# A layer norm's first root on ScalarE, a third gate tile in halves, and a moved y product, in a scan-plus-FFN kernel whose VectorE order comes from two virtual clocks

## The chip, the cores and the metric

The kernel runs on one core of a Trainium2 chip. The metric is the device time in microseconds (us) of the whole program; "span" is the time from the first to the last instruction in the hardware profile of one execution, some 2 us shorter than the device time. Engines are written as the profile has them: PE is TensorE, PEld its weight loads, DVE VectorE, ACT ScalarE, POOL GpSimd.

## The reference

```python
xn = layernorm(x)                                  # x: 1 x 2048 x 512, bf16
Bu = einsum("bld,pd->blp", xn, B_bar)              # complex
for t in range(2048):
    h = Lam_bar * h + Bu[:, t, :]                  # 512 complex states
y = 2 * real(einsum("blp,dp->bld", hs, C)) + xn * Dskip
f = (gelu(xn @ w_gate) * (xn @ w_up)) @ w_down     # 512 -> 1376 -> 512
return x + y * silu(f)
```

## The kernel before

The 2048 tokens are worked through in four slabs of 512. The complex scan is made real by rotating: VectorE multiplies the input `U` by cosine and sine tables (`pp`, `qq`, combined to `Wt`), scans in real arithmetic (`Ft`), and rotates back (`pp`, `qq`, combined to `hst`). TensorE then makes `y` of a 128-token block from `hst` and `C`, eight matmuls of 512 columns: the first four read the real half of `hst`, two per half of the states, so that the third matmul is the first to need states that were rotated last. TensorE executes in the order of the program; a slab is eleven "gate steps" (a gate tile and an up tile each), and the y of the slab before are put between certain gate steps.

The head of the kernel:

```python
dummies(9)                                    # TensorE warm-up matmuls, 512 columns each
pt_ps = psum.tile(...); nc.tensor.transpose(pt_ps, pv, ident)     # small parameters
dummies(5)                                    # five more
ACT(out=pf, in_=pt_ps, func=AF.Copy)
...
for m in range(2): bn(0, m)                   # VectorE: statistics of token blocks 0, 1
bn_end(0, 0); bn_end(0, 1)
rstd(0, 0, 2)                                 # VectorE: + eps; GpSimd: ** -0.5
bn(0, 2); bn(0, 3)
xs = [norm0(0), norm0(1)]
...
tps = [t_xn0(0, xs[0]), t_xn0(1, xs[1])]      # TensorE transposes of the normalised blocks
xnT_out(nc.vector, 0, tps[0])                 # copies out of PSUM
xnT_out(nc.scalar, 1, tps[1], 0, KT // 2)
xnT_out(nc.vector, 1, tps[1], KT // 2, KT)
SPLIT = 2                                     # gate/up tiles 0 and 1 are made in token halves
```

And the layer that decides VectorE's order. It keeps two virtual clocks while the program is written; an operation put into `later` is pulled out when the clock says that it fits before the next one:

```python
clk = {"pe": 0.0, "dve": 0.0}
waiting = []
def pe_takes(n, one=0.2157): clk["pe"] += n * one
def pop():
    r, c, f, _ = waiting.pop(0)
    clk["dve"] = max(clk["dve"], r) + c
    f()
def drain(t, late):
    while waiting and max(clk["dve"], waiting[0][0]) + waiting[0][1] <= t + late: pop()
def dve(ready, cost, f, late=0.8):
    drain(ready, late)                        # what fits goes ahead
    clk["dve"] = max(clk["dve"], ready) + cost
    f()
def later(ready, cost, f, key=None): waiting.append((ready, cost, f, key))
...
def ln_small(s):                              # four small statistics of slab 3
    def f(): ...
    dve(now() + 1.0, 0.3, f)
...
Y_AT = {1: (7, 8, 9, 10), 2: (2, 3, 4, 5), 3: (2, 4, 6, 8)}   # gate steps with a y
XN_AT = {1: 1, 2: 2}
clk["pe"] = 8.3                               # the two starting clocks
clk["dve"] = 10.6
```

## Time and profile before

| what | value |
|---|---|
| time, median of 6 runs | 184.6 us (184.21 to 184.93) |
| span of the profiled run | 182.5 us |
| TensorE busy | 175.9 us |
| VectorE busy | 168.0 us |
| TensorE's only wait for `hst` | 0.73 us, at the first y of slab 1 |

In a timeline a row is: start, length, engine, line, operation, output<-inputs, shapes and the number of instructions; brackets tell how long the engine was idle just before and what ended that. The prediction shows the main rows. One view that it doesn't show also belongs here, TensorE's timeline of the first 7 us of the kernel before:

```profile
1.18 3.99 PE L150 MATMUL w_ps<-warm 128*128 128x512 bf16 x9 [1.18 <-DVE halfpi L126]
...
5.21 1.25 PE L150 MATMUL w_ps<-warm 128*128 128x512 bf16 x5
6.39 0.72 PE L178 MATMUL tp<-ident,xn 128*128 128x128 bf16 x8
```

From 1.18 us to the first transposes at 6.39 this view shows no gap and names no wait, but it doesn't tell what the transposes stood behind, because ends of matmuls are modelled. Starts tell it. Five warm-ups of 0.216 from 5.21 on leave TensorE free at 6.29, and the transposes start 0.45 after the normalisation (5.94); in e8 below, where a wait for `xn` is named, the distance is 0.47. So the normalised block came last here, and the warm-ups were only 0.1 ahead of it: a block that is 0.42 earlier would have found TensorE still at its warm-ups.

### The profile page before, as it was taken

How to read it: one execution, taken by the hardware profiler on the slowest of the kernel's cores; microseconds unless marked ns; L12 is line 12 of the kernel's file. 1: busy time of each engine (PE TensorE's matmuls, PEld its weight loads, DVE VectorE, ACT ScalarE, POOL GpSimd, SP SyncE). 2: the span in 40 equal slices, each digit the busy share in tenths (PEclk: the TensorE clock that was granted, in tenths of full speed). 3: DMA queues.
4: the chain of work that ended last, by engine and by line, in shares of the span. 5: the costliest groups of instructions: out<-in, count | busy, mean ns of one | idle time of the engine just before them, and what ended most of it. 6: DMA issues, size and time to landing. Idle time of an engine off the chain costs nothing.

```text
span 182.5 us, 2411 instructions
## 1 busy us (share of the span) xinstructions
PE 175.9 (96%) x831; PEld 82.8 (45%) x847; DVE 168.0 (92%) x266; ACT 112.5 (62%) x196; POOL 18.5 (10%) x44
## 2 busy tenths in 40 slices
PE   7899999999999999999998999999999999999992
PEld 2564444544444444544443444444444444444451
DVE  4988899999998899999999999999999999999493
ACT  3199997778899943267889455767428444472200
POOL 3668300700000000000004000000000000000000
PEclk9999999999999999999999999999999999999999
DMA  5999595691001400023000032200000001000002
GB/s 146 323 356 157 93 239 105 184 252 31 0 0 29 81 5 32 29 64 108 0 0 4 29 83 63 57 2 4 0 0 0 0 29 34 29 29 0 0 29 86
DMA packets 25643, 12.37 MB, mean 68 GB/s; under 512 B 15808, under 2 KB 25632, under 8 KB 25632
## 3 DMA queue, kind: packets, MB, share of 16 engines
q1 hardware_dynamic: 25456, 12.16, 27.6%
q8 instruction: 6, 0.10, 0.2%
q10 hardware_dynamic: 176, 0.07, 0.1%
q14 instruction: 5, 0.04, 0.1%
HBM read 6.46 MB, written 2.10 MB: 47 GB/s over the span
## 4 chain that ended last, share of the span: by engine, by line
PE 60%; DVE 22%; ACT 8%; DMA 4%; SPq 3%; issue 1%
PE f_ps L478 16%; PE up_ps L231 12%; PE g_ps L231 12%; PE y_ps L493 10%; PE u_ps L377 9%; DVE Ft L423 5%; DMA x_tok<-in_A_x_dram 4%; DVE qq L393 3%; ACT xn L582 3%; DVE pp L393 3%; ACT ub L466 2%; ACT gt L465 2%; DVE hst L397 2%; DVE yg L515 2%; DVE Wt L397 1%; DVE st L158 1%
## 5 line engine op out<-in xcount | busy, mean ns | idle before, releaser
L231 PE MATMUL up_ps<-xnT,wu 128*128 128x512 bf16 (+2 forms) x184 | 45.5, 370 | 0.2
L231 PE MATMUL g_ps<-xnT,wg 128*128 128x512 bf16 (+2 forms) x178 | 44.8, 369 | 0.8 <-ACT xnT L199 0.5
L465 ACT ACTIVATE gt<-g_ps 128x512 bf16<-128x512 f32 (+1 forms) x44 | 27.1, 616 | 22.1 <-PE g_ps L231 18.1
L478 PE MATMUL f_ps<-wd,at 128*128 128x512 bf16 (+1 forms) x172 | 38.5, 379 | 0.2
L466 ACT ACTIVATE ub<-up_ps 128x512 bf16<-128x512 f32 (+1 forms) x44 | 27.2, 618 | 7.3 <-PE up_ps L231 7.3
L423 DVE TENSOR_TENSOR_SCAN Ft<-rho,it,Wt 128x512 bf16<-128x512 f32 x24 | 29.5, 1269 | 0.0
L493 PE MATMUL y_ps<-C,hst 128*128 128x512 bf16 x117 | 27.9, 379 | 0.7 <-DVE hst L397 0.6
L377 PE MATMUL u_ps<-xnT,BT 128*128 128x512 bf16 x125 | 28.3, 379 | 0.2
L231 PEld LDWEIGHTS <-wg 128*128 128x128 bf16 (+1 forms) x184 | 18.3, 100 | 20.4 <-issue 0.5
L231 PEld LDWEIGHTS <-wu 128*128 128x128 bf16 (+1 forms) x184 | 18.4, 100 | 19.6
L478 PEld LDWEIGHTS <-at 128*128 128x128 bf16 (+1 forms) x176 | 17.2, 98 | 20.8
L382 ACT ACTIVATE U<-u_ps 128x512 bf16<-128x512 f32 x32 | 19.0, 615 | 8.3 <-PE u_ps L377 8.3
L377 PEld LDWEIGHTS <-BT 128*128 128x128 bf16 x128 | 12.5, 98 | 15.0
L483 ACT ACTIVATE g<-f_ps 128x512 f32<-128x512 f32 x16 | 9.6, 598 | 14.6 <-PE f_ps L478 14.6
L493 PEld LDWEIGHTS <-hst 128*128 128x128 bf16 x120 | 11.7, 98 | 15.0 <-DVE hst L397 1.3
L471 DVE TENSOR_TENSOR at<-gt,ub 128x1024 bf16<-128x1024 bf16 x20 | 13.5, 679 | 0.6 <-ACT ub L466 0.6
L397 DVE TENSOR_TENSOR hst<-pp,qq 128x1024 bf16<-128x1024 bf16 x16 | 10.5, 689 | 0.2
L397 DVE TENSOR_TENSOR Wt<-pp,qq 128x1024 bf16<-128x1024 bf16 x16 | 10.5, 688 | 0.2
L158 DVE BATCH_NORM_STATS2 st<-x_tok 128x6 f32<-128x512 bf16 x12 | 7.5, 682 | 3.4 <-DMA x_tok<-in_A_x_dram 3.3
L582 ACT ACTIVATE xn<-x_tok,nb,rs 128x512 bf16<-128x512 bf16 x12 | 10.3, 859 | 0.0
L515 DVE TENSOR_TENSOR yg<-yt,g 128x512 bf16<-128x512 f32 x14 | 9.7, 692 | 0.6
L393 DVE TENSOR_TENSOR pp<-U,cos_b 128x2048 bf16<-128x2048 bf16 x8 | 9.8, 1223 | 0.2
(111 smaller groups left out, 152.7 us busy)
## 6 DMA issues: line engine op xcount, KB each, us to landing
out_dram<-ot SPq DMA_DIRECT2D x15, 128.0 KB, 1.7
x_tok<-in_A_x_dram SPq DMA_DIRECT2D x3, 512.0 KB, 5.4
wd<-in_B_w_down_dram SPq DMA_DIRECT2D x1, 1280.0 KB
wg<-in_B_w_gate_dram SPq DMA_DIRECT2D x2, 384.0 KB
wu<-in_B_w_up_dram SPq DMA_DIRECT2D x2, 384.0 KB, 6.7
wg<-in_B_w_gate_dram SPq DMA_DIRECT2D x1, 352.0 KB
wu<-in_B_w_up_dram SPq DMA_DIRECT2D x1, 352.0 KB, 4.0
x_tok<-in_A_x_dram SPq DMA_DIRECT2D x2, 128.0 KB, 2.2
```

What stands on the lines that cost most here:

```text
L231: nc.tensor.matmul(ps[:fs, a:b], lhsT=w[:, kt, fsl], rhs=xnT[:, kt, s * TS + a : s * TS + b], start=(kt == 0), stop=(kt == KT - 1),)
L377: nc.tensor.matmul(u_ps[:, :], lhsT=BT[:, ri, kt, pt * P : (pt + 1) * P], rhs=xnT[:, kt, cols], start=(kt == 0), stop=(kt == KT - 1),)
L382: ACT(out=U[:, ri, q, :], in_=u_ps[:, :], func=AF.Copy)
L393: TT(out=box[key][:], in0=src()[:], in1=tab[:, hs, :].unsqueeze(1).to_broadcast(W), op=ALU.mult)
L397: return lambda: TT(out=dst()[i], in0=box["pp"][:, i, :, :], in1=box["qq"][:, 1 - i, :, :], op=op)
L423: nc.vector.tensor_tensor_scan(out=box["F"][:, ri, q, :], data0=rho[:, pt : pt + 1].to_broadcast([P, TS]), data1=box["W"][:, ri, q, :], in ...
L465: ACT(out=gt[:fs, i, :], in_=g_ps[:fs, :], func=AF.Gelu_apprx_tanh)
L466: ACT(out=ub[:fs, i, :], in_=u_ps[:fs, :], func=AF.Copy)
L471: dve(now() + lag, 0.63, lambda: TT(out=at[:, j - 1 : j + 1, :], in0=gt[:], in1=ub[:], op=ALU.mult))
L478: nc.tensor.matmul(f_ps[:, :], lhsT=at[:fs, k, m0 : m0 + P], rhs=wd[:fs, k, :], start=(k == 0), stop=(k == NFT - 1))
L493: nc.tensor.matmul(y_ps[:, :], lhsT=hst[:, j // NPT, j % NPT, m0 : m0 + P], rhs=C2[:, j // NPT, j % NPT, :], start=(j == 0), stop=((s, m) ...
L582: ACT(out=xn[:], in_=x_tok[:, s * M + m, :], func=AF.Identity, scale=rs[:, s, m : m + 1], bias=nb[:, s, m : m + 1])
```

## The change

The intent: get the first normalised blocks earlier (a root on ScalarE and a reciprocal on VectorE in place of a power on GpSimd), give TensorE more work on the first half of the tokens (`SPLIT` 3), and let the y of slab 1 wait less for `hst` (one gate step later). The loads were reordered to suit, and the two starting clocks set anew.

```diff
-    CUTS = (0, 2 * P, 5 * P, 8 * P, F)
+    CUTS = (0, 2 * P, 4 * P, 8 * P, F)
...
     load_gu(0)
+    load_gu(1)
     load_x(1)
-    load_gu(1)
...
-    ACT(out=tiny[:], in_=halfpi[:], func=AF.Sin)
+    ACT(out=tiny[:], in_=halfpi[:], func=AF.Sqrt)
...                                    (eps and sd tiles)
-    rstd(0, 0, 2)
+    ACT(out=sd[:], in_=mv[:, 0, 0:2, 1], func=AF.Sqrt, bias=eps[:])
+    ACT(out=tiny[:], in_=halfpi[:], func=AF.Sin)
+    ACT(out=pf[:], in_=pt_ps[:, :], func=AF.Copy)
+    bn(0, 2)
+    nc.vector.reciprocal(out=rs[:, 0, 0:2], in_=sd[:])
     nc.gpsimd.tensor_tensor(out=dt_[:], in0=euler[:], in1=ldt, op=ALU.pow)
-    bn(0, 2)
+    xs = [norm0(0), norm0(1)]
+    tps = [t_xn0(0, xs[0]), t_xn0(1, xs[1])]
+    xnT_out(nc.vector, 0, tps[0])
+    xnT_out(nc.scalar, 1, tps[1])
     bn(0, 3)
-    xs = [norm0(0), norm0(1)]
     bn_end(0, 2)
     bn_end(0, 3)
     rstd(0, 2, 4)
-    tps = [t_xn0(0, xs[0]), t_xn0(1, xs[1])]
-    xnT_out(nc.vector, 0, tps[0])
-    xnT_out(nc.scalar, 1, tps[1], 0, KT // 2)
-    xnT_out(nc.vector, 1, tps[1], KT // 2, KT)
     xs += [norm0(2), norm0(3)]
-    SPLIT = 2
+    SPLIT = 3
...
-            if j == 0 and up == 1:
+            if j == 2 and up == 0:
                 tps += [t_xn0(2, xs[2]), t_xn0(3, xs[3])]
...
-    Y_AT = {1: (7, 8, 9, 10), 2: (2, 3, 4, 5), 3: (2, 4, 6, 8)}
-    XN_AT = {1: 1, 2: 2}
+    Y_AT = {1: (7, 8, 9, 10), 2: (3, 4, 5, 6), 3: (2, 4, 6, 8)}
+    XN_AT = {1: 1, 2: 3}
...
-    clk["pe"] = 8.3
-    clk["dve"] = 10.6
+    clk["pe"] = 7.7
+    clk["dve"] = 11.5
```

More of the change, by code (lines that the diff above doesn't have):

```diff
@@ L138 @@
     tiny = consts.tile([P, 1], FP32, name="tiny")
-    ACT(out=tiny[:], in_=halfpi[:], func=AF.Sin)
+    ACT(out=tiny[:], in_=halfpi[:], func=AF.Sqrt)
+    eps = consts.tile([P, 1], FP32, name="eps")
+    nc.gpsimd.memset(eps[:], EPS)
+    sd = consts.tile([P, 2], FP32, name="sd")
     euler = consts.tile([P, NPT], FP32, name="euler")
@@ L194 @@
     dummies(5)
-    ACT(out=pf[:], in_=pt_ps[:, :], func=AF.Copy)
     def xnT_out(eng, m, tp, k0=0, k1=KT):
```

## The prediction

> **What bounds the kernel now.** I read the page's busy shares first, then the chain that ended last, then the timeline of each engine around every wait in that chain.
>
> ```profile
> PE 175.9 (96%) x831; PEld 82.8 (45%) x847; DVE 168.0 (92%) x266; ACT 112.5 (62%) x196; POOL 18.5 (10%) x44
> ...
> PE y_ps L493 <- DVE hst L397: 0.6, 1, 0.6
> ...
> PE g_ps L231 <- ACT xnT L199: 0.5, 1, 0.5
> ...
> PEld L231 <- DVE xnT L201: 0.3, 1, 0.3
> ```
>
> The first line is the page's, the others are of the list of waits: TensorE is the bound, and it waits only three times in earnest. From 10.1 us on, its timeline has one gap, before the first y of slab 1. VectorE runs beside it with almost no idle time from 21 to 171 us: a second bound, just in front of TensorE. Four times TensorE takes up the state hst that VectorE has just rotated; those are the places to check. In the timeline around the gap:
>
> ```profile
> 95.03 0.19 ACT L553 ACTIVATION_READ_ACCUMULATOR junk<-x_tok 128x1 f32 x1
> ...
> 95.72 0.16 DVE L559 SCALAR_TENSOR_TENSOR mq<-sx 128x4 f32<-128x4 f32 x1
> ...
> 98.65 1.29 DVE L397 TENSOR_TENSOR hst<-pp,qq 128x1024 bf16<-128x1024 bf16 x2
> ...
> 99.40 1.47 PE L493 MATMUL y_ps<-C,hst 128*128 128x512 bf16 x5 [0.57 <-DVE hst L397]
> ```
>
> The y begins at 98.24; its third matmul, due 2 x 0.216 later at 98.67, is the first to need the second half of hst, and comes at 99.40: 0.73 us lost. The head of the kernel, from its timeline:
>
> ```profile
> 4.73 1.29 DVE L158 BATCH_NORM_STATS2 st<-x_tok 128x6 f32<-128x512 bf16 x2
> 4.74 0.72 POOL L165 TENSOR_TENSOR rs<-ve,mhalf 128x2 f32<-128x2 f32 x1 [2.49 <-DVE ve L164]
> ...
> 5.94 0.72 DVE L169 TENSOR_SCALAR xn<-x_tok,mv,rs 128x512 bf16<-128x512 bf16 x2
> ...
> 7.58 0.71 PE L231 MATMUL g_ps<-xnT,wg 128*128 128x256 bf16 x4 [0.47 <-ACT xnT L199]
> ```
>
> GpSimd's power is done at 5.46, yet the normalisation starts at 5.94: it stands behind two statistics (4.73 to 5.94), not behind the power.
>
> **What the Trainium skill says.** "ScalarE: Activation LUTs", What it computes, advises Sqrt on ScalarE and then VectorE's reciprocal in place of Rsqrt, which is the change. Its section What ACT_TABLE_LOAD costs gives about 1283 ns for a load plus some 1380 ns of drain at each change of set; this trace agrees on the load (2.30 to 3.58, 11.42 to 12.70) but shows no drain: the next activation starts 0.01 us later. "PSUM — Partial Sum Buffer", Engine vs sequencer instructions, says that the ScalarE, VectorE and GpSimd queues are strictly first in, first out and that matmuls start in program order. The trace agrees (the norm behind the statistics above), and my working rests on it: an instruction moved in VectorE's order delays all behind it.
>
> **The change part by part: the head.** Removed: VectorE's add of eps and one power on GpSimd (0.72). Added: a root (one small activation, 0.20) and a reciprocal (0.17, as of inv), plus a table load of 1.28 that ends near 5.9, before ScalarE is needed at 6.7. Third statistics at 4.73 (they wait for the load of x: issue 1.64 + 3.1), reciprocal 5.34, norm 5.52 in place of 5.94. All after it follows 0.42 earlier; but the copy of the second block is now whole on ScalarE (0.60, not 0.38), so the first gate matmul starts at 7.15 - 0.42 + 0.60 + 0.05 = 7.38, in place of 7.58.
>
> The third gate tile in halves gives TensorE two groups of 0.44 to do before tokens 256 to 511 are there. But the fourth statistics, behind the copy of xnT, now end near 7.4; eps, power and norms follow at 7.70, 7.97 and 8.70 (7.83 before), and the copy of the third block at 8.70 + 1.81 = 10.51 ends 10.93 (10.06 before). TensorE has finished its six half groups and transposes at 7.38 + 6 x 0.44 + 0.45 = 10.45 and waits 0.5. Second halves from 10.98: the fourth tile starts at 10.98 + 6 x 0.44 = 13.62, before 13.60. **The head gains nothing.** ScalarE's sines and its first gelu come 0.87 later (13.58), but the fifth gate tile (15.3), first to need that PSUM buffer, has over 1 us to spare.
>
> **y of slab 1.** Moved from gate step 2 to 3, its third matmul is due 8 x 0.216 = 1.73 later. If VectorE kept its times, the 0.73 would be gone.
>
> **VectorE's new order.** The two starting clocks of the recording layer (7.7 and 11.5) reorder VectorE's queue. I compared both built orders at the four uses of hst, with times of before measured against TensorE's, so that a shift of everything cancels.
> - Slab 1, y of slab 0. The rotation pp (1.14) came before the fourth skip product z, and now stands behind it; z waits for ScalarE's last xn until 62.18. Then z 0.34 + pp 1.14 + at 0.60 + qq to hst 1.26 + hst 0.69 = 66.21, but the third matmul is due at 64.55 + 0.43 = 64.98. New wait: 1.28.
> - Slab 2, y of slab 1. The four small statistics of slab 3 used to stand behind all four scans, and now stand between two and two. They need ScalarE's last sum (95.22, now 96.50 with the 1.28). Before, they came at 95.72 and waited for nothing; now VectorE is there at about 95 and waits. From there: small 0.6, two scans and the carry 2.9, pp 1.14, at 0.60, qq 1.26, hst 0.69: 103.7. The third matmul is due at 98.67 + 1.73 + 1.28 = 101.68. New wait: 2.0 in place of 0.73.
> - Slab 3, y of slab 2: hst at 136 for a y at 141; several us to spare.
> - The end. Behind the last y product of slab 3 (y complete 158.73, three operations 1.79) there were left Wt, at, four scans, at, pp, qq, hst; now also pp, qq and a second Wt. From 160.56: pp 1.14, at 0.60, qq 1.14, at 0.31, Wt 1.21, scans 4.86, pp 1.14, qq 1.26, hst 0.69 = 172.9; the third matmul is due at 171.53 + 0.43 = 171.96. New wait: 1.0.
>
> Sum: 0.0 + 1.28 + (2.0 - 0.73) + 1.0 = +3.55 us, with few hundredths for eight more matmuls. 184.82 + 3.55 = 188.4. I take **188.1**, since one of the three waits may be shorter than added up.
>
> **The rivals.**
> 1. The intended gain. Head 0.2 to 0.6 earlier and y without its wait: 183.5 to 184.2. For it speaks the gap of 0.73 that is plainly there; against it VectorE's order, which holds TensorE at hst three times.
> 2. Neutral: VectorE absorbs the order because something that it waits for comes sooner, leaving only one of three waits: about 185.5. Against: each wait is worked out from an event of TensorE or ScalarE (xn, the sums, the last y), not from VectorE's backlog.
> 3. VectorE becomes the bound throughout: its backlog adds to the waits, 189 or more. For it: 92% busy. Against: its waits are for TensorE's own products, so that it catches up there.
>
> **Range and chances.** The three waits carry perhaps 0.4 each; if one is missing the time is near 187 or 186.5; if all hold with a late head, 189. The range is 186.2 to 189.2. The 2% border is 184.82 x 1.02 = 188.5, just above the sum: slower by over 2% 0.28, within 2% 0.69, faster by over 2% 0.03 (all waits of TensorE together are not 3.7 us).
>
> **What would show it.** Norm near 5.5 and first gate matmul near 7.4; second halves after 10.9 with a TensorE wait of about 0.5; fourth tile at 13.6. In the list of waits, TensorE for hst three times: near 65 (1.3), near 102 (2.0), at the end (1.0). VectorE idle near 62 for xn and near 95 for the accumulator. It is wrong if the tile after the second halves starts before 13.2, or if the y's have no wait: then the order costs nothing and rival 1 holds.

## The result, and the profile after

The kernel after takes 188.83 us (median of 6 runs, 188.07 to 188.99), against 184.6 before. The ratio is 1.0224, with a 95% interval of 1.02 to 1.0247: slower by 2.2%. A ratio here is the mean time of one kernel's fast runs over the mean of the other's of the same rounds, so it is not quite the ratio of the medians. The profiled spans are 182.5 and 186.3, a difference of 3.8 us; the other 0.4 of the 4.2 lies outside the span, where no trace looks (see the end of the section on the prediction).

The page's line of busy times in the kernel after:

```profile
PE 177.0 (95%) x855; PEld 83.4 (45%) x855; DVE 168.8 (91%) x265; ACT 113.8 (61%) x199; POOL 18.3 (10%) x44
```

TensorE and VectorE both do about 1 us more work than before, and not 3.8. (The change adds eight matmuls, and the trace of before lacks some: it shows 831 matmuls for 847 weight loads.) The list of waits (waiter, line, releaser: us in all, times, longest) tells the rest:

```profile
PEld L497 <- DVE hst L401: 5.0, 3, 2.1
PE y_ps L497 <- DVE hst L401: 3.5, 3, 1.6
```

There was one wait of matmuls for `hst` of 0.6 before, and there are three of 3.5 in all now. TensorE's timeline at each of the three, in the kernel after:

```profile
65.01 0.59 PE L497 MATMUL y_ps<-C,hst 128*128 128x512 bf16 x2
66.72 1.47 PE L497 MATMUL y_ps<-C,hst 128*128 128x512 bf16 x6 [1.11 <-DVE hst L401]
...
101.71 0.59 PE L497 MATMUL y_ps<-C,hst 128*128 128x512 bf16 x2
103.91 1.47 PE L497 MATMUL y_ps<-C,hst 128*128 128x512 bf16 x6 [1.61 <-DVE hst L401]
...
174.32 0.59 PE L497 MATMUL y_ps<-C,hst 128*128 128x512 bf16 x2
175.73 1.47 PE L497 MATMUL y_ps<-C,hst 128*128 128x512 bf16 x6 [0.82 <-DVE hst L401]
```

Two matmuls go, and the third waits. It was due 2 x 0.216 = 0.43 after the first, so the losses are 66.72 - 65.44 = 1.28, 103.91 - 102.14 = 1.77 and 175.73 - 174.75 = 0.98 us. What VectorE does ahead of the first two, from its timeline; the first row is of the kernel before, the others of the kernel after:

```profile
59.58 1.22 DVE L393 TENSOR_TENSOR pp<-Ft,cos_b 128x2048 bf16<-128x2048 bf16 x1
...
62.63 0.42 DVE L582 TENSOR_TENSOR z<-xn,Db 128x512 bf16<-128x512 bf16 x1 [0.46 <-ACT xn L586]
62.97 1.22 DVE L397 TENSOR_TENSOR pp<-Ft,cos_b 128x2048 bf16<-128x2048 bf16 x1
...
65.97 1.29 DVE L401 TENSOR_TENSOR hst<-pp,qq 128x1024 bf16<-128x1024 bf16 x2
...
96.24 0.16 DVE L563 SCALAR_TENSOR_TENSOR mq<-sx 128x4 f32<-128x4 f32 x1 [0.83 <-ACT junk L557]
96.32 0.17 DVE L564 TENSOR_SCALAR nm<-sx 128x4 f32<-128x4 f32 x1
96.99 0.16 DVE L565 SCALAR_TENSOR_TENSOR sx<-sx,mq 128x4 f32<-128x4 f32 x1 [0.51 <-ACT junk L557]
```

Near 62 the long rotation `pp` stands behind a small product that waits for ScalarE; near 96 VectorE, with two scans still to do, waits 0.83 and 0.51 for ScalarE's sums, for the sake of four operations of 0.16. Ahead of the third, the product of the last input rotation (`qq` from `U`) and the last of the three operations on the y of slab 2 (`ot`) have changed places. First the kernel before, then the kernel after:

```profile
157.12 1.22 DVE L393 TENSOR_TENSOR qq<-U,sin_b 128x2048 bf16<-128x2048 bf16 x1
...
160.43 0.42 DVE L516 TENSOR_TENSOR ot<-yg,x_tok 128x512 bf16<-128x512 bf16 x1
```

```profile
163.00 0.42 DVE L520 TENSOR_TENSOR ot<-yg,x_tok 128x512 bf16<-128x512 bf16 x1
...
165.08 1.22 DVE L397 TENSOR_TENSOR qq<-U,sin_b 128x2048 bf16<-128x2048 bf16 x1
```

At the head, TensorE's timeline of the kernel after reads:

```profile
1.17 4.02 PE L153 MATMUL w_ps<-warm 128*128 128x512 bf16 x9 [1.17 <-DVE halfpi L126]
...
5.25 1.36 PE L153 MATMUL w_ps<-warm 128*128 128x512 bf16 x5
6.44 0.61 PE L181 MATMUL tp<-ident,xn 128*128 128x128 bf16 x8
...
7.74 0.60 PE L235 MATMUL g_ps<-xnT,wg 128*128 128x256 bf16 x4 [0.69 <-ACT xnT L201]
```

The norm did come earlier (5.54 against 5.94), but the transposes start at 6.44 against 6.39, 0.90 after the norm: now they stand behind the fourteen warm-ups, the last five of which took 1.19 here (5.25 to 6.44). The fourth gate tile starts at 14.05 against 13.60, so the head lost 0.45. The sum 0.45 + 1.28 + (1.77 - 0.73) + 0.98 = 3.75 is the 3.8 of the spans.

### The profile page after: what moved, and what is told of

The parts are those of the page before. It is cut to its first block, busy times and chain, and to the rows that moved or that the text cites. A ratio compares the mean times of both kernels' runs of the same rounds, so it can differ in the third digit from the quotient of the medians.

```text
span 186.3 us, 2445 instructions
## 1 busy us (share of the span) xinstructions
PE 177.0 (95%) x855; PEld 83.4 (45%) x855; DVE 168.8 (91%) x265; ACT 113.8 (61%) x199; POOL 18.3 (10%) x44
## 4 chain that ended last, share of the span: by engine, by line
PE 78%; DVE 14%; ACT 6%; issue 0%
PE f_ps L482 15%; PE g_ps L235 15%; PE u_ps L381 15%; PE up_ps L235 15%; PE y_ps L497 13%; DVE Ft L427 4%; PE w_ps L153 3%; DVE pp L397 2%; DVE qq L397 2%; ACT xn L586 2%; ACT gt L469 1%; ACT ub L470 1%; DVE hst L401 1%; DVE at L475 1%; PE y_ps L534 1%; ACT junk L557 1%
## 5 line engine op out<-in xcount | busy, mean ns | idle before, releaser
L235 PE MATMUL g_ps<-xnT,wg 128*128 128x512 bf16 (+2 forms) x188 | 45.7, 365 | 1.1 <-ACT xnT L201 0.7
L497 PE MATMUL y_ps<-C,hst 128*128 128x512 bf16 x120 | 28.5, 379 | 3.5 <-DVE hst L401 3.5
L475 DVE TENSOR_TENSOR at<-gt,ub 128x1024 bf16<-128x1024 bf16 x20 | 13.6, 679 | 0.6 <-ACT ub L470 0.6
```

What stands on the lines that cost most here:

```text
L235: nc.tensor.matmul(ps[:fs, a:b], lhsT=w[:, kt, fsl], rhs=xnT[:, kt, s * TS + a : s * TS + b], start=(kt == 0), stop=(kt == KT - 1),)
L475: dve(now() + lag, 0.63, lambda: TT(out=at[:, j - 1 : j + 1, :], in0=gt[:], in1=ub[:], op=ALU.mult))
L497: nc.tensor.matmul(y_ps[:, :], lhsT=hst[:, j // NPT, j % NPT, m0 : m0 + P], rhs=C2[:, j // NPT, j % NPT, :], start=(j == 0), stop=((s, m) ...
```

## The experiments

**The theory** was that the two starting clocks reorder VectorE's queue, that this order holds TensorE in three places, each with its own cause, and that the moved y by itself gains and the head by itself loses a little. **The rivals:** VectorE's total work is the bound, so that any idle of VectorE is made up or lost elsewhere; or the head puts the later engines behind for good. Every ratio below is to the kernel before in the same rounds. Its median was 184.22 in the rounds of e1 to e4, 184.46 in those of e5 to e8 and 184.24 in those of e9 to e11.

### e1: the clocks alone

```diff
 (the kernel before)
-    clk["pe"] = 8.3
-    clk["dve"] = 10.6
+    clk["pe"] = 7.7
+    clk["dve"] = 11.5
```

> Kernel before with only the two starting clocks changed (7.7, 11.5), so only VectorE's order differs. Order theory: wait of TensorE for hst 1.28 us in slab 1, about 3.4 us in slab 2 (the hst ends near 103.4, and y still stands at gate step 2, its third matmul due at 99.95), about 1.0 us at the end, in place of 0.73: +5.0 us, 189.5 us, slower than the changed kernel. Rival, that the head's late VectorE work causes the loss: the head is as before here, so about 184.6 us.

Measured: 190.42 us (189.52 to 191.55), ratio 1.0336 [1.0304, 1.0368]. Two numbers that emit no instruction cost more than the whole change. In the profiled run the 1.7 us of slow matmuls (below) come on top of the waits. The list of waits:

```profile
PE y_ps L493 <- DVE hst L397: 5.3, 3, 3.3
```

The three waits are there. The one in slab 2 is now much longer (the y starts at 99.50, its third matmul at 103.43: 3.50 lost), since here the y isn't moved. The runs fall in two groups, with spans of 187.7 to 188.1 at a mean granted clock of 0.998 to 0.999, and of 189.2 to 189.8 at 0.991. The profiled run is of the second group, and TensorE's timeline shows why:

```profile
103.43 2.38 PE L493 MATMUL y_ps<-C,hst 128*128 128x512 bf16 x6 [3.33 <-DVE hst L397]
105.60 1.84 PE L231 MATMUL g_ps<-xnT,wg 128*128 128x512 bf16 x4
107.28 1.03 PE L231 MATMUL up_ps<-xnT,wu 128*128 128x512 bf16 x4
```

After this stop the matmuls ran slow, with a granted clock of 0.50 between 104 and 106 us: six took 2.17 from start to start, where six take 6 x 0.216 = 1.30, and the four after them 1.68 for 0.86. That is 1.7 lost by a wait that was itself 3.5. It can account for the distance of the two groups, 1.5 us between their mean spans, but no trace of the faster group was taken.

### e2: the moved y alone

```diff
 (the kernel before)
-    Y_AT = {... 2: (2, 3, 4, 5) ...};  XN_AT = {1: 1, 2: 2}
+    Y_AT = {... 2: (3, 4, 5, 6) ...};  XN_AT = {1: 1, 2: 3}
```

> Kernel before with only y of slab 1 and the normalisation of slab 3 moved to gate steps 3 to 6. Order theory: the third matmul is due 1.73 us later, the wait of 0.73 us for hst is gone, nothing else moves: 183.9 us. Rival, that the move of y disturbs VectorE's order in slab 2: 185 or more, with a wait for hst later.

Measured: 183.64 us (183.53 to 183.9), ratio 0.9968 [0.9955, 0.9981]. No matmul waits for `hst`. The chain that ended last, by engine, before and then in e2:

```profile
PE 60%; DVE 22%; ACT 8%; DMA 4%; SPq 3%; issue 1%
```

```profile
PE 97%; ACT 1%; DVE 1%; issue 0%
```

This part did what it was meant to, and the kernel is faster than both. In e2 the chain is almost nothing but TensorE; in the kernel after it is TensorE 78%, VectorE 14%, ScalarE 6%.

### e3: the head alone

```diff
 (the kernel after)
     clk and Y_AT, XN_AT back to those of the kernel before
```

> Kernel before with only the new head (root and reciprocal, third tile in halves, weights first), old clocks, old place of y. Theory: TensorE starts its fourth tile near 14.05 us in place of 13.60, all else moves along with it: +0.45 us, 185.05 us. Rival, that VectorE's start 1.3 us late is a debt that it cannot make up: waits for hst in slab 1 and 2 grow, +1.0 us or more.

Measured: 185.45 us (184.54 to 186.54), ratio 1.0071 [1.0043, 1.0099]; spans 182.5 to 183.4. The fourth gate tile starts at 14.20 in its trace, 0.60 later than before. The head alone loses 1.3 us in the mean, but only 0.5 of it within the span (183.0 against 182.45); the rest lies outside.

### e4: the kernel after with the old clocks

```diff
 (the kernel after)
-    clk["pe"] = 7.7;  clk["dve"] = 11.5
+    clk["pe"] = 8.3;  clk["dve"] = 10.6
```

> Changed kernel with the two starting clocks as before (8.3, 10.6). Order theory: all three waits for hst gone; +0.45 from the head, -0.73 from y: 184.3 us. Rival, head and y themselves carry part of the loss: 186 us or more.

Measured: 184.69 us (184.13 to 185.89), ratio 1.0029 [1.0002, 1.0056]; spans 182.0 to 183.1. No matmul waits for `hst`; what is left in the list is one weight load of 0.2. With the same instructions and the old order the loss, 4.2 us between the medians, is down to 0.5. Within the span nothing is lost (182.3 in the mean, 182.45 before). The clocks, that is the order, are the main cause.

### e5: one of the three causes alone

Only the four small statistics are moved, behind all four scans; VectorE's queue is otherwise that of the kernel after.

```diff
 (the kernel after, in ln_small)
-        dve(now() + 1.0, 0.3, f)
+        dve(now() + 3.0, 0.3, f)
```

> The kernel after with one number changed: the recording layer takes the four small statistics of slab 3 as ready 3.0 instead of 1.0 after TensorE's last product of the slab, so that they stand behind all four scans and the carry instead of between scans two and three. Nothing else in VectorE's queue changes (218 rows against 219, the same operations). Theory of the order: VectorE no longer idles for ScalarE's last sum there (0.83 + 0.51 = 1.34 us in the kernel after), so the wait of TensorE before the first y of slab 2 falls from 1.77 to about 0.4, the waits of slab 1 (1.28) and of the end (0.98) stay: 188.8 - 1.3 = 187.5, a ratio to the kernel before of about 1.016. Rival, VectorE's backlog (its total work sets the end, the idle is caught up later or lost elsewhere): unchanged, 188.8, ratio 1.023.

Measured: 187.45 us (187.1 to 188.24), ratio 1.0169 [1.0145, 1.0193]; span 185.4 against 186.3. VectorE's timeline, and after it TensorE's:

```profile
98.22 0.15 DVE L563 SCALAR_TENSOR_TENSOR mq<-sx 128x4 f32<-128x4 f32 x1
...
98.76 1.22 DVE L397 TENSOR_TENSOR pp<-Ft,cos_b 128x2048 bf16<-128x2048 bf16 x1
100.38 0.69 DVE L475 TENSOR_TENSOR at<-gt,ub 128x1024 bf16<-128x1024 bf16 x1 [0.40 <-ACT ub L470]
```

```profile
103.00 1.47 PE L497 MATMUL y_ps<-C,hst 128*128 128x512 bf16 x6 [0.91 <-DVE hst L401]
```

The idle of 1.34 for ScalarE's sums is gone, and `pp` starts at 98.76 instead of 100.17. But the next operation, the product `at`, then waits 0.40 for a gate tile, and `hst` comes 0.91 earlier, not 1.34. TensorE's loss is 103.00 - 102.15 = 0.85 in place of 1.77, and the span is 0.9 shorter: what VectorE gained reached the end in full. The direction was expected; the size, a wait of 0.4, was not, as a second producer stood close behind the first. The rival of VectorE's backlog expected no change, and falls.

### e6: VectorE's clock set back at slab 3

```diff
 (the kernel after)
     for s in range(NS):
+        if s == 3:
+            clk["dve"] -= 1.5
```

> The kernel after with the layer's VectorE clock set back by 1.5 at the start of slab 3: VectorE's order from slab 3 on is that of the kernel with the old starting clocks, slabs 0 to 2 keep the order of the kernel after. Theory of the order: the waits for hst near 65 (1.28) and near 102 (1.77) stay, that of the end falls from 0.98 to 0.1 or less: 188.8 - 0.9 = 187.9, ratio 1.018. Rival, one cause early in the kernel (the late head or slab 1 puts VectorE behind for good, so that the end waits whatever its order): end wait still near 1, 188.8.

Measured: 187.86 us (186.88 to 189.14), ratio 1.0191 [1.0156, 1.0226]. The list of waits:

```profile
PE y_ps L497 <- DVE hst L401: 2.9, 2, 1.8
```

The waits of slabs 1 and 2 are there, and that of the end is gone. The trace shows that the order isn't quite that of the old clocks, which the expectation says it is (several operations, `Wt` and `at` among them, stand elsewhere than in e4), but `pp` and `qq` of the last input (160.01 and 161.15) are ahead of the last operations on the y of slab 2 (from 162.29) again. So the wait was a matter of VectorE's order in slab 3, not of an engine that had fallen behind before. The ratio is 0.3% below that of the kernel after, with intervals that overlap; the verdict rests on the trace.

### e7, e8, e9, e11: the head, and the warm-ups ahead of it

The late transposes called for a test of the warm-ups. Four kernels, all with the old clocks and the moved y, vary the second group of warm-ups. e7 has two instead of five, e9 eight:

```diff
 (e4)
-    dummies(5)
+    dummies(2)          # e7;   dummies(8) in e9
```

e8 has two, and a head in another order; e11 is e8 with five:

```diff
 (e7)
     xs = [norm0(0), norm0(1)]
+    bn(0, 3)
...
     xnT_out(nc.scalar, 1, tps[1])
-    bn(0, 3)
...
-            if j == 2 and up == 0:
+            if j == 1 and up == 1:
                 tps += [t_xn0(2, xs[2]), t_xn0(3, xs[3])]
+                xnT_out(nc.vector, 2, tps[2])
                 xnT_out(nc.scalar, 3, tps[3])
...                                    (behind the angles)
-    xnT_out(nc.vector, 2, tps[2])
```

> The kernel after with the old starting clocks (as e4) and with two warm-up matmuls instead of five behind the transpose of the parameters. Theory: the five ran until about 6.3 in e4 and held TensorE's first transposes, whose xn was ready at about 5.96; with two they start at about 6.0, the first gate matmul comes at about 7.3 instead of 7.74, the fourth tile at about 13.5 instead of 13.84 in e4 and 14.05 in the kernel after; time 0.3 to 0.45 below e4, span about 181.7. Rival: the warm-ups are not what held the transposes (or the fourth statistics and the parameters behind it hold the second halves anyway): the fourth tile stays at 13.8 to 14.05 and the time is that of e4.

> e7 with the head put in another order as well: the fourth statistics ahead of the copy of the first xnT, the transposes of tokens 256 to 511 after four half groups instead of five, and the copy of block 2 straight behind the norms instead of behind the chain of angles. Expected from the times of the kernel after: first gate matmul about 7.4, norms of blocks 2 and 3 about 8.2, second halves with no wait at 7.4 + 6 x 0.44 + 0.45 = 10.5, fourth tile 13.1 against 13.60 before; TensorE has no wait for hst (the y of slab 1 moved, old clocks): about 0.5 + 0.7 below the kernel before, 183.1 to 183.5, ratio about 0.994, at or below e2. Rival: the sines and the first gelu, pushed back behind the copies, hold a PSUM buffer or VectorE's tables, and nothing is gained on e7.

> e4 (the kernel after with the old starting clocks) with eight warm-up matmuls instead of five behind the transpose of the parameters: the suspected cost made larger. Theory: TensorE works through its warm-ups without a gap from 1.2 us on, and the first transposes stand behind them in its queue; xn is ready at 5.9 to 6.1. Three more, at 0.22 to 0.43 each depending on when TensorE's matmuls become fast, start the transposes 0.65 to 1.3 later, and the first gate matmul, the fourth tile and the end follow: span 182.7 to 183.4 against about 182.3 of e4, ratio near 1.006. Rival: the head is held by the statistics and norms of blocks 2 and 3 and not by TensorE's queue: within 0.2 of e4.

> e8 with the five warm-up matmuls of the kernel after instead of two. If the queue of warm-ups holds the head's first transposes, they start 0 to 0.45 later than in e8 (6.05) depending on when TensorE becomes fast, fourth tile 13.1 to 13.6, time 0.1 to 0.4 above e8: ratio 0.996 to 0.998. If the order of the copies was all that mattered in e8: the same 0.996.

Measured:

| run | warm-ups | time, us | ratio to before | mean span, and less that of before in the same rounds | norm, then transposes start, profiled run |
|---|---|---|---|---|---|
| e7 | 9 + 2 | 184.1 | 0.998 [0.9963, 0.9997] | 182.0, -0.7 | 5.72, 6.19 |
| e4 | 9 + 5 | 184.69 | 1.0029 [1.0002, 1.0056] | 182.3, -0.15 | 5.76, 6.23 |
| e9 | 9 + 8 | 185.48 | 1.0063 [1.004, 1.0086] | 183.05, +0.6 | 5.49, 7.92 |
| e8 | 9 + 2, new order | 183.7 | 0.9959 [0.9941, 0.9978] | 181.65, -1.1 | 5.58, 6.05 |
| e11 | 9 + 5, new order | 184.73 | 1.0025 [0.9996, 1.0053] | 182.2, -0.3 | 5.41, 7.24 |

TensorE's timelines of the heads of e8, e9 and e11, in this order:

```profile
4.84 0.60 PE L153 MATMUL w_ps<-warm 128*128 128x512 bf16 x2
6.05 0.72 PE L181 MATMUL tp<-ident,xn 128*128 128x128 bf16 x8 [0.61 <-DVE xn L172]
```

```profile
5.25 2.83 PE L153 MATMUL w_ps<-warm 128*128 128x512 bf16 x8
7.92 0.61 PE L181 MATMUL tp<-ident,xn 128*128 128x128 bf16 x8
```

```profile
5.25 2.15 PE L153 MATMUL w_ps<-warm 128*128 128x512 bf16 x5
7.24 0.61 PE L181 MATMUL tp<-ident,xn 128*128 128x128 bf16 x8
```

In e8 the transposes wait for `xn`, as they should. In e9 and e11 nothing is named: they stand behind the warm-ups, 2.43 and 1.83 after the norm. In e11 VectorE normalised at 5.41, the earliest of all. A warm-up takes 0.43 or 0.22 from start to start, and when it turns from the one to the other differs between runs: five took 1.19 in the kernel after (5.25 to 6.44) and 1.99 in e11 (5.25 to 7.24).

So e8 and e11 differ in the turn as well as in the number: the first nine took 3.56 in e8 and 3.96 in e11. Traces with like turns keep the two apart. Where the turn came early, five warm-ups held nothing: in e6, with the head of the kernel after, the nine took 3.45 and the transposes start at 6.06, 0.47 after the norm, as in e8 with two. Where it came late, they held much: e11 starts its transposes at 7.24 and its first gate matmul at 8.54, and e7, with two, at 6.19 and 7.88. So the head is held by the warm-ups in some runs and not in others. Over all runs the means show a cost: e9's span is 0.75 above e4's, and e11's, each against before in its own rounds, 0.8 above e8's. (Three of e11's six spans, 181.7 to 181.8, lie among those of e8.) The repaired order of e8, with its fourth gate tile at 13.14 (13.60 before), is worth something only where the warm-ups let it through.

e7 missed its expectation in the trace: the fourth tile came at 14.01, not 13.5. The transposes start at 6.19, 0.47 after the norm, but so they do in e4 (6.23 after 5.76): the expectation had e4's `xn` ready at 5.96, and in that trace the five warm-ups held nothing. And in e7's trace TensorE was still slow at the transposes (a median of 314 ns each, against 219 in the kernel after), which took from 6.19 to 7.2; with so few warm-ups the slow phase lasted past them in that run. Its time did fall: the ratios of e7 and e4 have intervals that don't overlap, and its mean span is 0.7 below that of before in the same rounds, e4's 0.15. e8 and e11 missed too: 183.7 us for 183.1 to 183.5, and a ratio of 1.0025 for 0.996 to 0.998, with the fourth tile at 14.22 for 13.1 to 13.6, as e11's warm-ups turned fast later than expected.

### e10: clocks and y, without the head

```diff
 (the kernel before)
     clk 7.7 and 11.5;  Y_AT, XN_AT as in the kernel after
```

> The kernel before with the new starting clocks and the moved y, and its old head: what is left of the change without the head. If VectorE's order is the whole cause of the loss beyond the head: waits for hst of about 1.3, 1.8 and 1.0, span 185.9 to 186.3 (182.5 + 1.28 + 1.77 - 0.73 + 0.98 = 185.8, head as before), time 187.8 to 188.4, ratio about 1.020. Against e1 (y not moved: ratio 1.034) the moved y then saves about 1.7 us, its eight matmuls. Rival, the new head is part of the loss in the later slabs (its later gelu puts ScalarE and VectorE behind): 186 or less.

Measured: 187.64 us (187.53 to 188.14), ratio 1.0193 [1.0179, 1.0208]; span 185.8: both a little under the ranges expected. TensorE's three waits:

```profile
66.22 1.47 PE L493 MATMUL y_ps<-C,hst 128*128 128x512 bf16 x6 [1.11 <-DVE hst L397]
...
103.42 1.47 PE L493 MATMUL y_ps<-C,hst 128*128 128x512 bf16 x6 [1.60 <-DVE hst L397]
...
175.25 4.92 PE L493 MATMUL y_ps<-C,hst 128*128 128x512 bf16 x22 [0.83 <-DVE hst L397]
```

They are those of the kernel after to 0.01 (1.11, 1.61, 0.82), each about 0.5 earlier. The head shifts everything behind it and plays no part in the waits; the rival that it puts other engines behind falls. The difference of the ratios, 1.0224 - 1.0193 = 0.0031, or 0.6 us, with intervals that overlap, is what the head adds. The time outside the span is 0.4 longer in the kernel after than in e10 (2.17 against 1.80 in the mean), so a part of it is in no trace.

### The parts together

| kernel | clocks | y | head | ratio |
|---|---|---|---|---|
| e2 | old | moved | old | 0.9968 |
| e3 | old | old | new | 1.0071 |
| e4 | old | moved | new | 1.0029 |
| e1 | new | old | old | 1.0336 |
| e10 | new | moved | old | 1.0193 |
| after | new | moved | new | 1.0224 |
| e8 | old | moved | repaired | 0.9959 |

Moving y is worth 0.3 to 0.4% with the old clocks and 1.4% with the new ones. There it takes the wait in slab 2 from 3.50 to 1.77, 0.9% of the time; the rest can be e1's slow stretch after that wait, 1.7 us in the one trace and perhaps in half of its runs. e2 and e8 both beat both kernels. They ran in different rounds, and their intervals overlap, so which of them is better is open. The head's own parts (the root, the third tile in halves, the order of the loads) were not run apart.

## Why the prediction was right and where it was not

**The range held, the likelier class did not.** The time of 188.83 lies in 186.2 to 189.2, 0.7 above the 188.1 named. The outcome is slower by over 2%, to which the prediction gave 0.28, and 0.69 to "within 2%". Its sum was 188.4, and its border 188.5. It then took 0.3 off, "since one of the three waits may be shorter than added up". One was, by 0.23, but the head was later by 0.43, and some 0.4 more came outside the span, on which the text has nothing. That the number came as close as 0.7 is in part luck, as these errors have both signs. An allowance on one side only was the poorest step of the text. (The sums for slab 1 and the end, as shown, give 1.23 and 0.95; the 1.28 and 1.0 contain the 0.05 from the end of `hst` to the matmul.)

**The head, "gains nothing": wrong, it lost 0.45.** The norm at 5.5 was right (5.54), and the wait of about 0.5 before the second halves was (0.46; the view names ScalarE's `sh`, but the copy of the third block, 10.95 to 11.37, ends just before 11.42). The step that failed is "all after it follows 0.42 earlier". The transposes did not follow, because TensorE's own queue in front of them was busy until 6.44. The text cited the rule that matmuls start in program order, and then used it for VectorE's queue only. By the trace of before the same queue is free at 6.29, so that only 0.1 of the 0.42 could have come through; in the trace of after the warm-ups turned fast later, and nothing came. By the distance of 0.47 the transposes would have started at 6.01; the 0.43 that they lost is what all later times of the head slip by: first gate matmul 7.74 for 7.38, norms of blocks 2 and 3 at 9.13 for 8.70, second halves 11.42 for 10.98, fourth tile 14.05 for 13.62. The rest of the working holds, and e6 shows it: there the same head was not held by its warm-ups, and these times are 7.47, 8.76, 11.05 and 13.68. Even so the head gained nothing.

**Slab 1, 1.28: right,** 1.28 measured. VectorE's idle near 62 for `xn` is there. But the place of `z` is not the whole of it: the last scan before `pp` moved too, from 57.50 to 59.62. Without `z` and its wait `pp` could have started at about 62.1, an estimate from the end of the carry, which is 0.87 of the 1.28. No run takes this wait away by itself; that it comes with the clocks is shown by e1 and e4.

**Slab 2, 2.0: right in kind, 1.77 in size.** The working put all four small statistics, 0.6, behind ScalarE's last sum. Two of them need only an earlier sum and ran inside the wait (96.24 and 96.32), so only 0.28 came after 96.99. e5 shows this cause by itself.

**The end, 1.0: right,** 0.98 measured; e6 takes it away alone.

**The moved y: right.** "If VectorE kept its times, the 0.73 would be gone": e2 keeps them, and it is gone.

**Rivals.** The intended gain did not come, though e2 shows that a part of the change has it (183.64 lies in its 183.5 to 184.2). The neutral one, 185.5, would need two waits absorbed, and none was. VectorE as the bound throughout falls with e5 and e4: with nearly the same VectorE work (168.8 us busy in the kernel after, 167.6 in e4) the time differs by 4 us.

**Left open.** The time outside the span isn't constant, and it goes with the head: 1.73 to 1.85 us in every run of the kernels with the old head (before, e1, e2, e10), 2.0 to 3.4 in every run of those with the new one. So the new head costs 0.2 us at the least where no trace looks; which part of it does, no run tells. In the rounds of e1 to e4 and of e9 to e11 the new head's mean is 2.4 to 2.6, in those of e5 to e8 2.1 to 2.3, so ratios of new-head kernels from different rounds carry up to 0.4 us of this; the spans don't.

## What to carry to other kernels

When a list scheduler orders an in-order engine from estimated clocks, treat its constants as part of the code: compare the built queues ahead of every place where the bounding engine takes up a result, and look for a short instruction that waits for a slow third engine with long ones behind it. An early operand is worth nothing until the consumer's own queue lets it through, so read the consumer's rows before the first use too, warm-ups included, and by starts: a row that names no wait need not mean that the queue was full. Test a change of several parts part by part: here one part gained 0.6 us, and a pair of numbers beside it cost more than the whole.

## What the Trainium skill lacked or had wrong

- "TensorE: Matmul & The Clock Gate", What's actually happening, puts the turn to full speed at some 3.4 us of activity in a free-running window, varying by 500 ns, and in a further note says that the number of slow matmuls varies between runs. The traces agree that it varies, and by more: the slow warm-ups of 0.43 start at 1.17 or 1.18 in every run, and the turn, as an estimate from five warm-ups lasting 1.99 in e11 (4.2 slow ones of 0.43, the rest at 0.22) and nine lasting 3.45 in e6 (7.0 slow ones), comes at 7.1 us in the one and at 4.2 in the other.
- The same section advises against fitting the ramp, as a penalty below 1% of a span. The size agrees (e11 against e8 is 0.7% of the time, 0.8 us of the span), but it lacks what follows for the order of a queue: warm-ups that outlast the wait they fill hold the real work. In two runs with a late turn the transposes started at 6.19 with 9 + 2 of them (e7) and at 7.24 with 9 + 5 (e11), with `xn` coming earlier in the second case.
- The same section has the slow state return after an idle window of some 3.4 us. The trace of e1 agrees: after a stop of 3.5 us matmuls ran at a granted clock of 0.50 and 1.7 us more were lost. Waits of 1.8 us in the kernel after did not do so.
- "ScalarE: Activation LUTs", What ACT_TABLE_LOAD costs, adds some 1380 ns of drain to a load of 1283. The load agrees (4.78 to 6.06 in the kernel after), and no drain shows: the next activation starts at 6.08.
- "TensorE: Matmul & The Clock Gate", Seeing it yourself, warns that clock events in a trace can be unreliable. For the start the first clock record of each trace, full speed, stands where its matmuls turn fast, at 4.03 us in e6, 5.50 in the kernel after and 7.12 in e11. Before its first record a trace says nothing, and the query of the granted clock prints 1.00 there (e11, 4.5 to 6.5 us, warm-ups of 0.43 each): that reading is the tool's, and the durations must be read.
